# Joining the last scores of layer 0 with an AV operation, in a four-layer attention and GLU kernel with a written-out order

## The chip, the cores and the metric

The kernel runs on one core of a Trainium2 chip. The metric is the time of one execution on the device, in microseconds (us), as the median of several runs. The engines are TensorE (PE), VectorE (DVE), ScalarE (ACT), GpSimd (POOL) and SyncE (SP), which here only issues DMAs.

## The reference

Four residual layers run over x of 2048 rows by 448 columns in bf16: attention A, GLU B, then A and B again with the same weights. A has 16 heads of 28 columns; each row attends to itself and to 7 earlier rows at a distance of 2, 4, ... 14 (kg and vg below are the gathered rows). F is 1792.

```python
x = x + _A_ref(_layernorm(x, axis=-1), A_wqkv, A_wo)
x = x + _B_ref(_layernorm(x, axis=-1), B_w_gate, B_w_up, B_w_down)
x = x + _A_ref(_layernorm(x, axis=-1), A_wqkv, A_wo)
x = x + _B_ref(_layernorm(x, axis=-1), B_w_gate, B_w_up, B_w_down)

...
def _A_ref(x, wqkv, wo):
    ...
    logits = jnp.einsum("bhsd,bhswd->bhsw", q, kg) * scale
    logits = jnp.where(mask[None, None, :, :], logits, -1e9)
    attn = _softmax(logits, axis=-1)
    o = jnp.einsum("bhsw,bhswd->bhsd", attn, vg)
    return (lambda x, *d: x.transpose(*d))(o, 0, 2, 1, 3).reshape(B, S, D) @ wo
...
def _B_ref(x, w_gate, w_up, w_down):
    g = jnp.einsum("bsd,df->bsf", x, w_gate)
    u = jnp.einsum("bsd,df->bsf", x, w_up)
    h = g * u
    return jnp.einsum("bsf,fd->bsd", h, w_down)
```

## The kernel before

**Names.** The layers are li = 0 (A), 1 (B), 2 (A) and 3 (B). The rows are stored as 16 blocks of 128, four to a chunk. Even rows come first and odd rows after them, so that a distance of 2 becomes a distance of 1 and a window is a narrow band. Attention works on nine groups of queries per layer: group 0 is one query block, groups 1 to 8 are two query blocks of 120 each.

**One chunk of layer A.** Layer norm runs on DVE and ACT (L763 to L784) and gives `xn_sb`. A transpose by SP's DMA queue (L787) makes `xnTa`; in the first chunks PE does it (L794), with a copy out of PSUM (L801). Q and K are four units of 28 matmul halves (L834, tile `WQK`), copied to `qk` by ACT or DVE (L895). The last unit's columns are spread to their places by small DMAs `qk<-qk`, except in two chunks of layer 0. V is made in the same way (L834, tile `WV`), copied at L948.

**One group.** The scores are 64 small matmuls (L981) into four PSUM banks. ACT takes the exponential in two halves (L993), DVE multiplies by the band's mask (L1002), and AV is 64 small matmuls (L1020) into two banks. DVE and ACT then form the reciprocal of the row sums (L1044 to L1050, tile `R_sb`), and DVE normalises into `oT` (L1070), which gives AV's banks back. Two blocks of output projection (L854 with `wo_g`, called Y) and the addition to x (L1114) follow. In layer 2 a part of the heads is moved first by DMAs `oT<-oT`, and Y is L1106.

**One chunk of layer B.** After layer norm and transposes into `xnTb`, fourteen GLU units follow. Each is 14 matmuls (L1144) into one pair of banks; ACT copies g out (L1150) and DVE multiplies it with u (L1153) into `hT`. The down projection is 28 matmuls for two blocks (L854 with `WD`, L1165 at the very end), and DVE adds to x.

**PSUM.** There are eight banks. Nearly all operations take them in pairs and hold them until the copy, exponential, normalisation or addition that reads them has ended.

**The order.** `build` records about 1,400 operations with their dependencies in a `Sched`. The table `ORDER` has a list of operation numbers for each of PE, ACT, DVE, POOL and SP; `schedule` follows each list, one operation after the other, and hands out the banks, taking the pair that has been free longest. It also decides by its own model of time which banks those are. `emit` then writes the instructions with a wait on a semaphore for each dependency that crosses engines. Nothing overtakes on an engine: what is first in a list and not ready holds up all behind it. An operation that both ACT and DVE can do (a copy out of PSUM) is done by the one in whose list it stands.

**Tilings of PE.** Most matmuls use 64-row tiles in pairs; scores and AV use smaller tiles. Each stretch of scores or AV between other matmuls is called a visit to the small tiling.

**Joint operations.** `JOINT` has a tuple of groups for layer 0 and one for layer 2. If a group is listed, `a_chunk` does not record its AV at once, but records it together with the scores of the next group in one PE operation, by `pe_joint`: first 64 score matmuls, then 64 AV matmuls. It takes six banks together (four for the scores, two for AV) before it starts, and waits for what either part needs. In layer 2 eight groups are joined so; in layer 0 none.

Of the kernel before, what the change touches and what calls it, by code (L numbers as in the profile page):

```python
# [69 lines left out]
    ],  # L70
    "act": [
# [12 lines left out]
    ],  # L84
    "dve": [
# [19 lines left out]
    ],  # L105
    "pool": [
        23, 22, 24, 32, 19, 25, 26, 27, 18, 33, 28, 21, 20, 29, 30, 31, 34, 35, 36, 37,
    ],
# [8 lines left out]
    ],  # L117
}
ATT_P = 0.6
S_EST = 237.0  # L120
AV_EST = 241.0
A_CAP = 6
JOINT = ((), tuple(range(8)))
BPAIR = True
RESERVE = ("SV",)
RESERVE_P = 0.0
B_CAP = 8
SEQ = "A00 A01 B10 A02 B11 A03 B12 A20 B13 A21 B30 A22 B31 A23 B32 B33".split()

# [1180 lines left out]
```

## Time and profile before

| | us |
|---|---|
| median of 3 runs | 393.72 |
| lowest and highest run | 392.11 and 393.86 |
| the profiled execution | 391.6 |
| its span in the profile | 389.9 |
| PE busy in the span | 379.3 |
| DVE busy in the span | 263.8 |
| ACT busy in the span | 184.0 |

A row of a timeline has the start, the length, the engine, the line, the operation, the output and input tiles, the shapes and the number of instructions. In square brackets stand the idle time ahead of it and what ended that. Consecutive rows of the same kind are merged. The length of a row of matmuls includes the modelled end of the last one, so the distance from one row's start to the next row's start says how long the work took. A matmul of 512 columns takes about 108 ns, one of 448 columns about 94 ns, one of the small tiles about 10 ns.

### The profile page before, as it was taken

How to read it: one execution, taken by the hardware profiler on the slowest of the kernel's cores; microseconds unless marked ns; L12 is line 12 of the kernel's file. 1: busy time of each engine (PE TensorE's matmuls, PEld its weight loads, DVE VectorE, ACT ScalarE, POOL GpSimd, SP SyncE). 2: the span in 40 equal slices, each digit the busy share in tenths (PEclk: the TensorE clock that was granted, in tenths of full speed). 3: DMA queues.
4: the chain of work that ended last, by engine and by line, in shares of the span. 5: the costliest groups of instructions: out<-in, count | busy, mean ns of one | idle time of the engine just before them, and what ended most of it. 6: DMA issues, size and time to landing. Idle time of an engine off the chain costs nothing.

```text
span 389.9 us, 12779 instructions
## 1 busy us (share of the span) xinstructions
PE 379.3 (97%) x5694; PEld 201.2 (52%) x5694; DVE 263.8 (68%) x579; ACT 184.0 (47%) x302; POOL 6.0 (2%) x24
## 2 busy tenths in 40 slices
PE   7898999999999999999999999999999999999997
PEld 5454555555444555545444674445545555555554
DVE  6898879789897657355894278955478857733513
ACT  4996874772561336475143465332577303332310
POOL 6000000000000000000000000000000000000000
PEclk9999999999999999999999999999999999999999
DMA  7959675013142262000072000180001050310002
GB/s 218 266 104 159 98 128 134 3 26 74 25 72 59 30 87 57 11 6 5 5 108 43 14 6 5 24 126 5 12 2 45 19 96 13 79 41 2 13 0 96
DMA packets 53630, 22.59 MB, mean 58 GB/s; under 512 B 44288, under 2 KB 52648, under 8 KB 53576
## 3 DMA queue, kind: packets, MB, share of 16 engines
q1 hardware_dynamic: 52856, 21.15, 28.4%
q8 instruction: 45, 0.74, 0.8%
q10 hardware_dynamic: 720, 0.63, 0.5%
q14 instruction: 9, 0.07, 0.1%
HBM read 8.53 MB, written 1.84 MB: 27 GB/s over the span
## 4 chain that ended last, share of the span: by engine, by line
PE 90%; ACT 3%; DVE 3%; DMA 2%; issue 1%; SPq 1%
PE ps L1144 43%; PE ps L854 23%; PE ps L834 15%; PE ps L1106 3%; PE ps L1020 2%; PE ps L981 2%; PE ps L1165 1%; PE ps L683 1%; DMA xnTb<-xn_sb 1%; DMA qk<-qk 1%; DVE x_sb L1114 1%; ACT g_sb L1150 1%; ACT qk L895 1%; ACT E_sb L993 1%; SPq L619 1%
## 5 line engine op out<-in xcount | busy, mean ns | idle before, releaser
L1144 PE MATMUL ps<-xnTb,WGU 64*128 64x512 bf16 x1568 | 176.5, 376 | 0.8 <-DMA xnTb<-xn_sb 0.3
L1144 PEld LDWEIGHTS ps<-xnTb,WGU 64*128 64x128 bf16 x1568 | 81.1, 94 | 87.0 <-issue 4.2
L1150 ACT ACTIVATE g_sb<-ps 128x512 bf16<-128x512 f32 x112 | 64.9, 594 | 106.4 <-PE ps L1144 95.6
L1153 DVE TENSOR_TENSOR hT<-g_sb,ps 128x512 bf16<-128x512 bf16 x112 | 74.4, 681 | 51.2 <-ACT g_sb L1150 49.7
L854 PE MATMUL ps<-WD,hT 64*128 64x448 bf16 x840 | 85.7, 349 | 0.1
L854 PEld LDWEIGHTS ps<-WD,hT 64*128 64x128 bf16 x840 | 44.1, 94 | 34.6 <-DVE hT L1153 0.8
L1114 DVE TENSOR_TENSOR x_sb<-x_sb,ps 128x448 bf16<-128x448 bf16 x62 | 36.0, 614 | 30.0 <-PE ps L854 24.6
L834 PE MATMUL ps<-xnTa,WQK 64*128 64x512 bf16 (+1 forms) x448 | 47.2, 357 | 1.3 <-ACT E_sb L993 1.2
L993 ACT ACTIVATE E_sb<-ps 128x1024 bf16<-128x1024 f32 (+1 forms) x36 | 33.7, 980 | 17.9 <-PE ps L981 17.7
L763 DVE BATCH_NORM_STATS2 st<-x_sb 128x6 f32<-128x448 bf16 x64 | 38.2, 613 | 3.0 <-DMA x_sb<-in_A_x_dram 2.9
L784 DVE TENSOR_SCALAR xn_sb<-x_sb,mv,rstd 128x512 bf16<-128x512 bf16 (+1 forms) x64 | 34.8, 567 | 1.7 <-DMA xnTb<-xn_sb 1.0
L834 PEld LDWEIGHTS ps<-xnTa,WQK 64*128 64x128 bf16 x448 | 22.1, 94 | 23.0 <-ACT E_sb L993 2.7
L834 PE MATMUL ps<-WV,xnTa 64*128 64x448 bf16 (+1 forms) x252 | 28.1, 340 | 1.2 <-ACT lnv L766 0.8
L895 ACT ACTIVATE qk<-ps 128x1024 bf16<-128x1024 f32 (+1 forms) x24 | 22.8, 967 | 12.5 <-PE ps L834 12.4
L1070 DVE TENSOR_TENSOR oT<-ps,R_sb 128x448 bf16<-128x448 f32 (+2 forms) x38 | 21.1, 598 | 9.5 <-ACT R_sb L1050 9.5
L1002 DVE TENSOR_TENSOR E_sb<-E_sb,MK 128x1024 bf16<-128x1024 bf16 (+2 forms) x40 | 23.5, 604 | 3.3 <-ACT E_sb L993 3.2
L948 ACT ACTIVATE v_sb<-ps 128x896 bf16<-128x896 f32 (+1 forms) x16 | 13.7, 868 | 20.5 <-PE ps L834 20.4
L1049 ACT ACTIVATE R_sb<-R_sb 128x960 f32<-128x960 f32 (+1 forms) x18 | 17.3, 959 | 7.7 <-DVE R_sb L1047 7.5
L766 ACT ACTIVATE lnv<-mv,eps_sb 128x2 f32<-128x2 f32 (+1 forms) x34 | 9.2, 292 | 20.2 <-DVE mv L765 19.9
L834 PEld LDWEIGHTS ps<-WV,xnTa 64*128 64x128 bf16 x252 | 12.7, 94 | 11.2 <-issue 1.2
L1050 ACT ACTIVATE R_sb<-R_sb 128x960 f32<-128x960 f32 (+1 forms) x18 | 17.3, 959 | 0.4
L981 PEld LDWEIGHTS ps<-qk 28*64 28x64 bf16 x1088 | 10.1, 103 | 9.8 <-issue 4.8
(47 smaller groups left out, 172.6 us busy)
## 6 DMA issues: line engine op xcount, KB each, us to landing
out_dram<-x_sb SPq DMA_DIRECT2D x15, 112.0 KB, 1.8
WGU<-in_B_w_gate_dram SPq DMA_DIRECT2D x7, 224.0 KB, 5.1
WGU<-in_B_w_up_dram SPq DMA_DIRECT2D x7, 224.0 KB, 4.3
WD<-in_B_w_down_dram SPq DMA_DIRECT2D x14, 112.0 KB, 2.6
x_sb<-in_A_x_dram SPq DMA_DIRECT2D x3, 448.0 KB, 5.9
hT<-in_A_wqkv_dram SPq DMA_DIRECT2D x3, 224.0 KB, 5.0
qk<-qk SPq DMA_DIRECT2D x24, 28.0 KB
xnTb<-xn_sb SPq DMA_TRANSPOSE x32, 3.2
```

The lines of the kernel that those rows point to most:

```text
L763: sc.add("dve", one(lambda E, B=B: E.bn_stats(st6[:, B, :], x_sb[:, B, :]), ("bn", li, B)), 525.0, deps=[("x", li - 1, B)] + ([("xn", li - ...
L784: sc.add("dve", one(lambda E, B=B, dst=dst, src=src: E.tensor_scalar(dst, src, mv[:, B, 0:1], rstd[:, B:B + 1], ALU.subtract, ALU.mult), ( ...
L834: ins.append((lambda E, w=w, c=c, lo=lo, st=st, sp_=sp_: E.matmul(u["out"](w), u["lhs"](w, c, lo, lo + 64), u["rhs"](w, c, lo, lo + 64), s ...
L854: ins.append((lambda E, w=w, c=c, lo=lo, st=st, sp_=sp_: E.matmul(outs(w), lhs(w, c, lo), rhs(w, c, lo), start=st, stop=sp_), keys[w] if s ...
L895: return E.activation(dst, src, ACT.Copy) if hasattr(E, "activation") else E.tensor_copy(dst, src)
L993: return E.activation(E_sb[:, slot, 2 * hp:2 * hp + 2, 0:w], ps[:, b0:b0 + 2, 0:w], ACT.Exp, scale=SCALE)
L1002: return E.tensor_tensor(e, e, m, ALU.mult)
L1070: return E.tensor_tensor(dst, src, rec, ALU.mult)
L1114: sc.add("dve", one(lambda E: E.tensor_tensor(x_sb[:, B, :], x_sb[:, B, :], ps[:, bk[w], 0:D], ALU.add), ("x", li, B)), dve_est(D), deps=[ ...
L1144: ins.append((lambda E, u=u, k=k, w=w: E.matmul(u["out"](w), WGU[64 * w:64 * w + 64, k, 128 * u["fc"]:128 * u["fc"] + 128], X[64 * w:64 * ...
L1150: sc.add("act", one(lambda E, gs=gs, bk=bk: E.activation(g_sb[:, gs, 0:n], ps[:, bk[0], 0:n], ACT.Copy), ("G", li, jp, fc)), act_est(n), d ...
L1153: sc.add("dve", one(lambda E, gs=gs, bk=bk, fc=fc: E.tensor_tensor(hT[:, fc, hs, h0:h1], g_sb[:, gs, 0:n], ps[:, bk[1], 0:n], ALU.mult), ( ...
```

## The change

Group 7 of layer 0 is listed in `JOINT`, so that AV of group 7 and the scores of group 8 become one operation. The number of operations falls by one, and all five lists of `ORDER` are replaced. No matmul is added or removed.

```diff
-JOINT = ((), tuple(range(8)))
+JOINT = ((7,), tuple(range(8)))
...
     "pe": [
-        280, 277, 281, 278, 283, 391, 261, 262, 392, 300, 288, 395, 397, 396, 393, 398, 394, 407, 305, 408, 296, 410, 297, 523, 411, 527, 524, 521, 528,
+        280, 277, 281, 278, 283, 391, 261, 392, 262, 300, 288, 395, 397, 396, 398, 393, 394, 305, 407, 296, 408, 297, 410, 523, 411, 527, 524, 521, 528,
...
```

Where it moves instructions is shown by rows of each engine's program, in order; "x" and a number at the end is how many alike stand in a row.

The first place is SP's queue between the loads of the weights and the Q/K work of chunk 2 of layer 0. L787 is the transpose of one block of that chunk, `WGU` are halves of the GLU weights (224 KB), `wo_g` pieces of the output projection (98 KB). Before:

```order
L619 DMA wo_g<-in_A_wo_dram 28x4x448
L787 DMA_TRANSPOSE xnTa<-xn_sb 128x4x128
L619 DMA WGU<-in_B_w_up_dram 64x1792
L787 DMA_TRANSPOSE xnTa<-xn_sb 128x4x128 x2
L619 DMA WGU<-in_B_w_up_dram 64x1792
L787 DMA_TRANSPOSE xnTa<-xn_sb 128x4x128
L619 DMA WGU<-in_B_w_up_dram 64x1792
```

Now:

```order
L619 DMA WGU<-in_B_w_up_dram 64x1792
L787 DMA_TRANSPOSE xnTa<-xn_sb 128x4x128
L619 DMA wo_g<-in_A_wo_dram 28x4x448
L619 DMA WGU<-in_B_w_gate_dram 64x1792 x2
L619 DMA wo_g<-in_A_wo_dram 28x4x448
L787 DMA_TRANSPOSE xnTa<-xn_sb 128x4x128 x3
L619 DMA WGU<-in_B_w_gate_dram 64x1792 x2
```

Four loads now stand between the first transpose and the three others, which follow each other directly; before, one load stood behind the first and one ahead of the last.

The second place is PE behind the scores of group 2 of layer 0 (the first row of each piece). `WQK` is Q and K of chunk 2, `wo_g` two blocks of Y. Before:

```order
L981 MATMUL ps<-qk 64x64 x64
L834 MATMUL ps<-xnTa,WQK 128x512 x6
L854 MATMUL ps<-wo_g,oT 128x448 x16
L834 MATMUL ps<-xnTa,WQK 128x512 x8
L981 MATMUL ps<-qk 64x64 x64
L1020 MATMUL ps<-E_sb,v_sb 32x64 x64
```

Now:

```order
L981 MATMUL ps<-qk 64x64 x64
L834 MATMUL ps<-xnTa,WQK 128x512 x6
L854 MATMUL ps<-wo_g,oT 128x448 x8
L834 MATMUL ps<-xnTa,WQK 128x512 x8
L854 MATMUL ps<-wo_g,oT 128x448 x8
L981 MATMUL ps<-qk 64x64 x64
L1020 MATMUL ps<-E_sb,v_sb 32x64 x64
```

The two halves of Y stood next to each other; now eight Q/K matmuls stand between them.

The third place is PE around the joint operation. `WD` are down matmuls, L1144 GLU units, L981 scores and L1020 AV; the last rows of scores and AV of layer 0 are among them. Before:

```order
L854 MATMUL ps<-WD,hT 128x448 x14
L1144 MATMUL ps<-xnTb,WGU 128x512 x14
L854 MATMUL ps<-WD,hT 128x448 x28
L981 MATMUL ps<-qk 64x64 x64
L1144 MATMUL ps<-xnTb,WGU 128x512 x42
L1020 MATMUL ps<-E_sb,v_sb 32x64 x64
L1144 MATMUL ps<-xnTb,WGU 128x512 x70
```

Now:

```order
L854 MATMUL ps<-WD,hT 128x448 x14
L981 MATMUL ps<-qk 64x64 x64
L1144 MATMUL ps<-xnTb,WGU 128x512 x14
L854 MATMUL ps<-WD,hT 128x448 x28
L981 MATMUL ps<-qk 64x64 x64
L1020 MATMUL ps<-E_sb,v_sb 32x64 x64
L1144 MATMUL ps<-xnTb,WGU 128x512 x42
L1020 MATMUL ps<-E_sb,v_sb 32x64 x64
L1144 MATMUL ps<-xnTb,WGU 128x512 x70
```

Scores of group 8 are followed by AV of group 7 without anything between them; scores of group 7 come later than before, behind the down matmuls.

Some copies out of PSUM change their engine. In layer 2, four of Q/K (two of chunk 0, one each of chunks 1 and 3) and four of V go from ACT to DVE, and two of Q/K of chunk 3 from DVE to ACT; in the head, one copy of a transpose goes from DVE to ACT, and of four copies that arrange the Q/K weights two go each way.

More of the change, by code (lines that the diff above doesn't have):

```diff
@@ L55 @@
     "pe": [
[14 rows of a table removed]
[14 rows of a table added]
     ],
     "act": [
[12 rows of a table removed]
[11 rows of a table added]
     ],
     "dve": [
[19 rows of a table removed]
[20 rows of a table added]
     ],
     "pool": [
-        23, 22, 24, 32, 19, 25, 26, 27, 18, 33, 28, 21, 20, 29, 30, 31, 34, 35, 36, 37,
+        21, 24, 32, 28, 33, 29, 23, 25, 26, 22, 27, 19, 34, 35, 30, 31, 20, 18, 36, 37,
     ],
     "sp": [
[7 rows of a table removed]
[7 rows of a table added]
     ],
```

102 rows, old and new, of the table ORDER are left out of this document.

## The prediction, made before the result was known

> **What bounds the kernel now.** I read the page first (engine totals, slices, chain), then PE's and SP's timelines, then the rows around each place where the order changes.
>
> ```profile
> span 389.9 us, 12779 instructions
> PE 379.3 (97%) x5694; PEld 201.2 (52%) x5694; DVE 263.8 (68%) x579; ACT 184.0 (47%) x302; POOL 6.0 (2%) x24
> PE 90%; ACT 3%; DVE 3%; DMA 2%; issue 1%; SPq 1%
> ```
>
> PE is busy for 379.3 of 389.9 us and 90% of the chain. The joint operation issues the same 64 score and 64 AV matmuls as before, so PE's work doesn't shrink. What can move is its idle time, 389.9 - 379.3 = 10.6 us, and what hides inside busy time: slower matmuls at a change of tiling, and waits shorter than a matmul. The table of stretches says where the idle time lies (length, then PE, PEld, DVE and ACT busy):
>
> ```profile
> 0.00:20.00 20.00, 16.56 (x310) 9.78 (x312) 15.48 (x49) 13.73 (x30) 6.04 (x24) 1.00 0.90 241
> 20.00:40.00 20.00, 18.06 (x427) 9.06 (x425) 18.15 (x50) 16.23 (x25) 0.00 (x0) 1.00 0.75 129
> 40.00:56.00 16.00, 15.69 (x335) 8.32 (x333) 12.94 (x35) 12.71 (x17) 0.00 (x0) 1.00 0.75 110
> 80.00:112.00 32.00, 31.84 (x544) 16.46 (x542) 28.49 (x60) 15.33 (x25) 0.00 (x0) 1.00 0.27 48
> 286.00:295.00 9.00, 8.14 (x279) 4.50 (x279) 7.04 (x17) 7.42 (x9) 0.00 (x0) 1.00 0.04 11
> ```
>
> Before 20 us PE waits for loads, which keep their order up to the weights of layer 0. From 20 to 56 us 1.94 + 0.31 = 2.25 us are idle, with ACT and DVE close to full; where the join is put (80 to 112) only 0.16. So the join has little to win by itself, and the new order of the first 56 us has more.
>
> **The change part by part.** *Transposes of chunk 2 (28 to 33 us).* These PE and SP rows carry the largest term; the view of xnT in that window adds, last, the time of its transposes to landing; the last row is of the page's DMA issues.
>
> ```profile
> 30.38 0.84 PE L981 MATMUL ps<-qk 28*64 28x64 bf16 x64 [0.46 <-DVE v_sb L948]
> 32.37 0.82 PE L834 MATMUL ps<-xnTa,WQK 64*128 64x512 bf16 x6 [1.15 <-ACT E_sb L993]
> 33.02 1.94 PE L854 MATMUL ps<-wo_g,oT 64*128 64x448 bf16 x16
> 34.79 1.03 PE L834 MATMUL ps<-xnTa,WQK 64*128 64x512 bf16 x8
> 21.88 1.29 SPq L787 DMA_TRANSPOSE xnTa<-xn_sb  x1
> 27.57 0.59 SPq L619 DMA_DIRECT2D WGU<-in_B_w_up_dram  x1
> 28.21 2.41 SPq L787 DMA_TRANSPOSE xnTa<-xn_sb  x1
> DMA to landing us min/median/max: 2.5/4.3/5.8
> WD<-in_B_w_down_dram SPq DMA_DIRECT2D x14, 112.0 KB, 2.6
> ```
>
> The scores of group 2 need 0.64 us (a score row further below runs from 102.47 to 103.11), so PE is through at 30.38 + 0.64 = 31.02 and stands until 32.37: 1.35 us. The row names ACT's exp, but that had no part in it: the operation that starts there is the first Q of chunk 2, and the last input it needs is the transpose issued at 28.21, behind the load of 27.57, 4.16 us before, near the median of 4.3. In the new order one transpose goes at about 21.9, then four loads of 0.6 each, then the other three back to back: 21.9 + 1.3 + 4 x 0.6 = 25.6, and at 1.3 each the third is issued at about 28.2, with no load between. It lands 2.5 us later (the shortest of the row) at 30.7, 4.3 us later at 32.5, or 5.8 us later at 34.0. PE, itself about 0.35 late from the head (by ACT's rows taken in the new order: copies of T now stand behind a Q copy of 1.0), gets there at 31.02 + 0.35 = 31.37. The first Q would so start at 31.4, 32.5 or 34.0, against 32.37. The 5.8 is that of a transpose with four loads of 224 KB just ahead of it; here the four are two of 224 and two of 98 KB, and the third transpose has two others in front of it, which give the loads 2.6 us to drain. I take 31.6: **-0.75** with the head in it, bounds -1.0 and +1.6.
>
> [...]
>
> *Y halves and the first GLU unit (33 to 56 us).* The 16 matmuls of L854 above take 34.79 - 33.02 = 1.77 us, two halves of 8 that write one pair of banks, where 16 such matmuls need 1.51 at 94.5 ns each (14 take 280.28 - 278.95 = 1.33 in the rows on bank waits below): 0.26 lost. The new order puts eight Q matmuls between them: **-0.25** (bounds -0.26, 0). The stretch ends at a transpose:
>
> ```profile
> 51.55 4.01 DMA xnTb<-xn_sb
> 54.75 0.74 PE L834 MATMUL ps<-WV,xnTa 64*128 64x448 bf16 x6
> 55.80 1.47 PE L1144 MATMUL ps<-xnTb,WGU 64*128 64x512 bf16 x12 [0.31 <-DMA xnTb<-xn_sb]
> ```
>
> Between the V of 54.75 (6 steps of 94.5 = 0.57, so done at 55.32) and the GLU unit of 55.80 lie 0.48 us, for the last of four xnTb transposes. They now follow the qk copies directly, and the Y and x additions behind them come earlier by what was won above, so the wait doesn't come back whole: **-0.3** (bounds -0.5, 0). Together 0 to 56: **-1.3**.
>
> *Around the join (74 to 110 us).*
>
> ```profile
> 96.56 1.49 PE L854 MATMUL ps<-WD,hT 64*128 64x448 bf16 x14
> 98.21 1.69 PE L1144 MATMUL ps<-xnTb,WGU 64*128 64x512 bf16 x14 [0.16 <-ACT rstd L768]
> 99.73 2.81 PE L854 MATMUL ps<-WD,hT 64*128 64x448 bf16 x28
> 102.47 0.71 PE L981 MATMUL ps<-qk 28*64 28x64 bf16 x64
> 103.11 4.71 PE L1144 MATMUL ps<-xnTb,WGU 64*128 64x512 bf16 x42
> 107.75 0.68 PE L1020 MATMUL ps<-E_sb,v_sb 64*32 64x64 bf16 x64
> ```
>
> Joining saves one visit to the small tiling. 28 down matmuls ahead of scores take 102.47 - 99.73 = 2.74 us, 28 x 94.5 ns are 2.64: 0.10 a visit. **-0.10**. 14 down matmuls need 1.32, so PE is free at 97.88 and waits 0.33 for a transpose until 98.21; that one is issued earlier now: **-0.33** (bound 0). Against it: the joint operation takes six of the eight banks at once (scores two pairs, AV one), so the second GLU unit behind it waits until its exp or its x addition frees a pair: +0.17, from 0 to +1.0 (one pass of ACT over a pair of banks, as in rival C). And it can't start before the masked exp of group 7, whose second half ACT now does behind a G copy; by the ACT and DVE rows it is ready at about 101.45, PE is there at 101.5. No wait is counted; what is queued behind it is the whole of PE. With +0.06 for two down halves set next to each other: **-0.2** (bounds -0.45, +1.0).
>
> *Bank waits in GLU units.* A unit that follows only one other since its banks' owner waits for the chain G copy, H multiply:
>
> ```profile
> 247.34 16.95 PE L1144 MATMUL ps<-xnTb,WGU 64*128 64x512 bf16 x154
> 264.11 5.48 PE L834 MATMUL ps<-xnTa,WQK 64*128 64x512 bf16 x56
> 277.43 1.69 PE L1144 MATMUL ps<-xnTb,WGU 64*128 64x512 bf16 x14
> 278.95 1.49 PE L854 MATMUL ps<-WD,hT 64*128 64x448 bf16 x14
> 280.28 0.73 PE L834 MATMUL ps<-WV,xnTa 64*128 64x448 bf16 x6
> ```
>
> A free unit takes 278.95 - 277.43 = 1.52; eleven in a row 264.11 - 247.34 = 16.77, 0.15 above 11 x 1.51, one such wait. Following the new order bank by bank, one of these goes (near 70 us), and four come (two in layer 1, two in layer 3): **-0.15 + 0.60** (bounds -0.15, +0.9).
>
> *Copies that change engine.* Most PSUM copies that move go from ACT to DVE, among them the first two Q/K casts of layer 2:
>
> ```profile
> 132.04 1.82 DVE L895 CAST qk<-ps 128x512 bf16<-128x512 f32 x2 [1.22 <-PE ps L834]
> 133.78 1.38 DVE L784 TENSOR_SCALAR xn_sb<-x_sb,mv,rstd 128x896 bf16<-128x896 bf16 x2
> 139.48 1.15 DVE L1114 TENSOR_TENSOR x_sb<-x_sb,ps 128x448 bf16<-128x448 bf16 x2 [4.33 <-PE ps L854]
> 141.84 0.34 PE L981 MATMUL ps<-qk 28*64 28x72 bf16 x32
> 163.72 3.51 DMA qk<-qk
> ```
>
> Two casts of 1.2 us more go into a row behind which DVE had nothing to do for 4.33 us. The last cast ends at about 135; the last qk copy is issued by about 137.1 and lands 3.5 us later at 140.6, 0.7 before the scores of 141.84 - 0.5 need it. Cost **0**; without that cover it is one for one.
>
> *Layer 3, 286 to 295 us.*
>
> ```profile
> 290.09 1.68 PE L1144 MATMUL ps<-xnTb,WGU 64*128 64x512 bf16 x14
> 292.53 0.71 PE L981 MATMUL ps<-qk 28*64 28x64 bf16 x64 [0.77 <-ACT g_sb L1150]
> ```
>
> The unit of 290.09 should end at 291.6; the scores wait 0.93, to 292.53, for a normalisation that holds their banks. The new order puts a GLU unit straight behind the AV ahead of it, which waits 0.54 for a pair that an exp still reads, but this eats most of the 0.93: **+0.15** (bounds -0.3, +0.54).
>
> Sum: -1.3 - 0.2 - 0.15 + 0.60 + 0.15 = **-0.9**. The profiled execution took 391.6 with 1.7 around its span; 390.7 then, and the runs' median of 393.72 lies 2.12 above the profiled one, so **392.8**.
>
> **The rivals.**
>
> *A, late transposes, small gain.* The third transpose lands as late as now, 32.4, as batches behind loads do; then the first Q starts where it did, and only the later terms stay: -0.9 + 0.75 = about -0.1, **393.6**. For it: median 4.3. Against: no load between the three.
>
> *B, the searched order removes the waits of 20 to 56 us nearly all.* Those are the 2.25 us idle of the table and 0.26 within Y; with them gone, the join at its lower bound (-0.45) and half of the new bank waits not there, -2.5 - 0.45 + 0.15 = -2.8 against the profile, **390.9**. For it: ACT's and DVE's queues were both rearranged, and each wait there is short. Against: ACT is 81% busy from 20 to 40 us, and something has to wait for it.
>
> *C, slower: transposes behind the loads at 5.8 us.* At 34.0 the first Q is 1.6 late, and R of group 2, whose two passes now both stand ahead of a Q copy on ACT, holds that copy's banks for one pass more:
>
> ```profile
> 39.79 1.00 ACT L895 ACTIVATE qk<-ps 128x1024 bf16<-128x1024 f32 x1
> 40.69 0.99 ACT L1050 ACTIVATE R_sb<-R_sb 128x960 f32<-128x960 f32 x1
> ```
>
> That is +1.6 in place of -0.75 and 1.0 for the pass: -0.9 + 2.35 + 1.0 = +2.4, **396.2**. It decides from a landing later than 33.5 on. Against: transposes of 5.8 us had twice the bytes ahead. [...]
>
> **How the numbers follow.** The forecast 0.45, A 0.15, B 0.23, C 0.17. Faster by over 0.5% means under 391.75, slower over 395.7; within lies what a measurement of this kernel can't tell from no change. B gives 0.2 of faster and the forecast's lower edge 0.1: 0.30. C gives 0.13 of slower, and unlisted waits 0.03: 0.16. The rest, 0.54, is same. The forecast's own range, by its bounds, is 391.3 to 394.2; to leave 2 in 10 out the whole reaches from 390.4 (a little below B) to 395.4 (short of the full price of C).
>
> **What would show it.** The first Q of chunk 2 at 31.4 to 32.0 instead of 32.37 and no row of 16 matmuls at L854 near 33 (step one and two); the first GLU unit of L1144 at 54.2 to 54.9; one stretch of scores and AV back to back near 101 with a GLU unit after it whose successor waits under 0.3; DVE casts of qk near 132 to 135 and scores near 141 without a wait on qk; a wait under 0.6 at the scores near 292. Wrong is the forecast if the first GLU unit comes after 55.8, if the joint operation is waited for by more than 0.3, or if scores of layer 2 show a wait on qk beyond that at 167.36 now.

## The result, and the profile after

The changed kernel takes 394.27 us in the median of 20 runs (392.15 to 396.81), the kernel before, run beside it, 392.50 (391.36 to 394.52): a ratio of 1.0037 [1.0021, 1.0054]. A second comparison of the same two kernels, e9 below, gave 1.0014 [0.9997, 1.0031]. So the change costs between nothing and 2 us. A gain of 0.9 had been forecast; the time lies within the range given and within 0.5% of the kernel before, but on the other side of it.

The page of the changed kernel, its span and its engine totals:

```profile
span 391.5 us, 12764 instructions
PE 379.7 (97%) x5694; PEld 202.5 (52%) x5694; DVE 269.5 (69%) x584; ACT 179.9 (46%) x297; POOL 5.8 (1%) x24
```

The span is 1.6 us longer than before (391.5 - 389.9), and PE's busy time is 0.4 longer; the other 1.2 are idle time of PE. The table of stretches says where (length, then PE, PEld, DVE and ACT busy, as before):

```profile
20.00:40.00 20.00, 17.40 (x449) 9.20 (x436) 18.07 (x50) 16.45 (x27) 0.00 (x0) 1.00 0.79 131
40.00:56.00 16.00, 15.41 (x327) 8.11 (x326) 12.94 (x30) 12.18 (x17) 0.00 (x0) 1.00 0.70 102
80.00:112.00 32.00, 31.89 (x594) 16.33 (x573) 27.25 (x61) 16.25 (x25) 0.00 (x0) 1.00 0.24 46
```

From 20 to 56 us PE now idles 2.60 + 0.59 = 3.19 us, against 2.25 before. Around the join it idles 0.11, as little as before. PE's timeline shows the place:

```profile
32.50 0.82 PE L834 MATMUL ps<-xnTa,WQK 64*128 64x512 bf16 x6 [1.03 <-DMA xnTa<-xn_sb]
33.14 0.94 PE L854 MATMUL ps<-wo_g,oT 64*128 64x448 bf16 x8
33.90 1.04 PE L834 MATMUL ps<-xnTa,WQK 64*128 64x512 bf16 x8
34.76 0.94 PE L854 MATMUL ps<-wo_g,oT 64*128 64x448 bf16 x8
35.63 0.71 PE L981 MATMUL ps<-qk 28*64 28x64 bf16 x64
36.27 0.75 PE L1020 MATMUL ps<-E_sb,v_sb 64*32 64x64 bf16 x64
36.95 2.01 PE L834 MATMUL ps<-xnTa,WQK 64*128 64x512 bf16 x19
40.53 2.55 PE L834 MATMUL ps<-xnTa,WQK 64*128 64x512 bf16 x23 [1.57 <-issue]
```

The scores of group 3 start at 35.63, still 0.12 ahead of the kernel before (35.75, below). Then the 42 Q/K matmuls, one row of 4.68 us before, fall into 19 and 23 with 1.57 us between them, and the bracket names no engine, no tile and no DMA, only "issue". That is the row to stop at. The 23 read the same tiles as the 19, and the stop lies within a unit of 14, so missing data is unlikely. Before, the same row was whole, in PE's timeline of the kernel before:

```profile
35.75 0.71 PE L981 MATMUL ps<-qk 28*64 28x64 bf16 x64
37.00 4.68 PE L834 MATMUL ps<-xnTa,WQK 64*128 64x512 bf16 x42
```

What could be missing is the instructions. The page's table of DMA queues has a kind that it calls instruction; the larger of its two queues is q8 (packets, MB, share of the engines):

```profile
q8 instruction: 45, 0.74, 0.8%
```

0.74 MB in 45 packets are 16 KB each; PE's 5,694 matmuls and 5,694 weight loads over 45 packets are 253 instructions a packet. By this count the author takes q8 to bring PE's code, one block a packet; no record names what is in one. Windows cut around the stop catch a single packet. The table of queues of the changed kernel for 37.95 to 39.20 us:

```profile
q1 hardware_dynamic: 294, 0.07, 259.3%
q8 instruction: 1, 0.02, 6.0%
```

And of the kernel before for 36.95 to 38.15:

```profile
q1 hardware_dynamic: 493, 0.12, 149.2%
q8 instruction: 1, 0.02, 5.8%
```

The packets' own records give 37.98 to 39.17 in the changed kernel and 36.99 to 38.10 before. So the code came 1.0 us later in the span, and 1.1 later against the start of the scores of group 3. PE resumed 1.36 us behind its end. Queue q1, which carries SP's transposes and weight loads, has a share above 100% in both (259.3 and 149.2), so the times of its packets overlap. SP's timeline of the changed kernel ahead of that packet:

```profile
23.44 2.34 SPq L619 DMA_DIRECT2D WGU<-in_B_w_gate_dram  x2
25.82 0.58 SPq L619 DMA_DIRECT2D wo_g<-in_A_wo_dram  x1
26.44 4.66 SPq L787 DMA_TRANSPOSE xnTa<-xn_sb  x3
31.15 1.24 SPq L619 DMA_DIRECT2D WGU<-in_B_w_gate_dram  x2
32.43 1.88 SPq L619 DMA_DIRECT2D WGU<-in_B_w_up_dram  x3
```

Five halves of the GLU weights, 224 KB each, go out in one piece from 31.15 to 34.31. Before there were four, from 30.66 to 33.18, in SP's timeline of the kernel before:

```profile
30.66 0.59 SPq L619 DMA_DIRECT2D WGU<-in_B_w_up_dram  x1
31.30 0.60 SPq L619 DMA_DIRECT2D WGU<-in_B_w_gate_dram  x1
31.94 0.60 SPq L619 DMA_DIRECT2D WGU<-in_B_w_up_dram  x1
32.58 0.60 SPq L619 DMA_DIRECT2D WGU<-in_B_w_gate_dram  x1
```

The ledger of the two profiles, by PE's rows:

| place | before | after | change in this stretch |
|---|---|---|---|
| first Q of chunk 2 | 32.37 | 32.50 | +0.13 |
| scores of group 3 | 35.75 | 35.63 | -0.25 |
| end of the 42 Q/K matmuls behind them | 41.68 | 43.08 | +1.52 |
| first GLU unit | 55.80 | 57.03 | -0.17 |
| end of the span | 389.9 | 391.5 | +0.35 |

### The profile page after: what moved, and what is told of

It is laid out like the page before. It is cut to its first block, busy times and chain, and to the rows that moved or that the text cites. A ratio compares the mean times of both kernels' runs of the same rounds, so it can differ in the third digit from the quotient of the medians.

```text
span 391.5 us, 12764 instructions
## 1 busy us (share of the span) xinstructions
PE 379.7 (97%) x5694; PEld 202.5 (52%) x5694; DVE 269.5 (69%) x584; ACT 179.9 (46%) x297; POOL 5.8 (1%) x24
## 4 chain that ended last, share of the span: by engine, by line
PE 89%; DVE 4%; ACT 3%; DMA 2%; issue 1%; SPq 1%
PE ps L1144 41%; PE ps L854 24%; PE ps L834 14%; PE ps L1106 3%; PE ps L981 2%; PE ps L1020 2%; PE ps L683 1%; PE ps L1165 1%; DMA qk<-qk 1%; DMA xnTa<-xn_sb 1%; ACT xnTa L801 1%; DVE E_sb L1002 1%; DVE R_sb L1047 1%; DVE R_sb L1045 1%; ACT E_sb L993 1%
## 5 line engine op out<-in xcount | busy, mean ns | idle before, releaser
L1144 PE MATMUL ps<-xnTb,WGU 64*128 64x512 bf16 x1568 | 176.3, 376 | 1.6 <-ACT E_sb L993 0.5
L1144 PEld LDWEIGHTS ps<-xnTb,WGU 64*128 64x128 bf16 x1568 | 82.2, 94 | 86.3 <-issue 5.3
L834 PE MATMUL ps<-xnTa,WQK 64*128 64x512 bf16 (+1 forms) x448 | 47.3, 356 | 2.7 <-issue 1.6
L784 DVE TENSOR_SCALAR xn_sb<-x_sb,mv,rstd 128x896 bf16<-128x896 bf16 (+1 forms) x64 | 35.5, 574 | 2.5 <-ACT rstd L768 1.7
L834 PEld LDWEIGHTS ps<-xnTa,WQK 64*128 64x128 bf16 x448 | 22.5, 94 | 23.7 <-issue 3.4
L834 PE MATMUL ps<-WV,xnTa 64*128 64x448 bf16 (+1 forms) x252 | 28.3, 339 | 0.6 <-DVE hT L1153 0.3
L895 ACT ACTIVATE qk<-ps 128x1024 bf16<-128x1024 f32 (+1 forms) x22 | 21.4, 988 | 13.7 <-PE ps L834 13.6
L834 PEld LDWEIGHTS ps<-WV,xnTa 64*128 64x128 bf16 x252 | 12.1, 94 | 11.6 <-PE ps L834 1.6
L895 DVE CAST qk<-ps 128x1024 bf16<-128x1024 f32 (+1 forms) x10 | 10.1, 1008 | 9.9 <-PE ps L834 9.7
L948 ACT ACTIVATE v_sb<-ps 128x896 bf16<-128x896 f32 (+1 forms) x12 | 10.2, 851 | 13.6 <-PE ps L834 13.6
```

The lines of the kernel that those rows point to most:

```text
L784: sc.add("dve", one(lambda E, B=B, dst=dst, src=src: E.tensor_scalar(dst, src, mv[:, B, 0:1], rstd[:, B:B + 1], ALU.subtract, ALU.mult), ( ...
L834: ins.append((lambda E, w=w, c=c, lo=lo, st=st, sp_=sp_: E.matmul(u["out"](w), u["lhs"](w, c, lo, lo + 64), u["rhs"](w, c, lo, lo + 64), s ...
L895: return E.activation(dst, src, ACT.Copy) if hasattr(E, "activation") else E.tensor_copy(dst, src)
L1144: ins.append((lambda E, u=u, k=k, w=w: E.matmul(u["out"](w), WGU[64 * w:64 * w + 64, k, 128 * u["fc"]:128 * u["fc"] + 128], X[64 * w:64 * ...
```

## The experiments

PE's matmuls are counted from the program's start, the first being 0. The 19 Q/K matmuls end with number 728, and 729 is the late one. "Stop" below is the time from the start of 728 to that of 729; the two start together, at 0.00, in the profiles of e5, e7, e8 and e12, in which no stop is seen. "Code" is the start of the q8 packet ahead of it, the fifth in each profile, from the packets' records.

**First round: is it the head, the join, or the code?** *e1* keeps the change but has SP's first 45 DMAs in the order of before.

```diff
-"sp": ..., 190, 196, 97, 105, 110, 102, 104, 214, 216, 210, 212, 103, ...
+"sp": ..., 192, 110, 101, 108, 109, 214, 210, 216, 103, 212, ...
```

> The changed kernel with the first 45 DMAs of SP's queue (weights, transposes and qk copies of layer 0, transposes of the first chunk of layer 1) in the order that they had before; all else as changed. Theory (late code): PE stops for 1.6 us inside the Q/K of chunk 2 because the load of its next instructions, asked for at about 35 us, stands behind the five weight loads that SP now issues in one piece; with the old queue it starts 1 us earlier and the stop shrinks to under 0.6 us: 1.0 to 1.5 us faster than the changed kernel, about 1.001 of the kernel before. Rival (banks): the stop is for banks held by the Q/K copy that ACT now does behind both passes of R of group 2; then it stays and the time stays at 1.004 of before. Rival (later order): the loss is behind 60 us; then nothing changes here either.

Measured: 398.34 us, ratio 1.0139 [1.0109, 1.0169]. The stop was gone, but the run says little: the first Q waited far longer for its transposes, as PE's timeline shows,

```profile
36.12 1.47 PE L776 MATMUL ps<-xnTa,WQK 64*128 64x512 bf16 x6 [4.11 <-DMA xnTa<-xn_sb]
```

(L776 is the L834 of the other listing; the experiments' order tables take fewer lines). SP's old order asks for blocks of `xn_sb` in an order in which the new DVE list doesn't make them: the first transpose of chunk 2 went out at 26.57, where it had gone at 21.48. A miss, and a reminder that one engine's list can't be swapped alone.

*e2* puts 24 short matmuls more into PE's warm-up (5,718 matmuls and as many weight loads in its page), which shifts all later code by 48 instructions against the work and touches no order.

```diff
+        if n == WARM + FILL - 1:
+            ins = [... matmul of 64 columns on the warm-up tile ... for k in range(24)] + ins
```

> The changed kernel with 24 more matmuls of 64 columns in the last warm-up operation at about 11 us, whose result nobody reads; all orders as changed. It moves every later instruction of PE by 48 places against the blocks in which code is loaded. Late code: the block's end comes before the scores of group 2, where PE stands for transposes anyway, so the next load is asked for 2 us or more earlier against the work; the stop of 1.6 us near 39 us goes, and at most 0.6 us are paid for the 24 matmuls: 0.8 to 1.6 us faster than the changed kernel, about 1.000 of before. Banks, or later order: the stop stays where it is in the work (behind 19 Q/K matmuls), and the time is that of the changed kernel or up to 0.6 us more.

Measured: 395.27 us, 1.0058 [1.0033, 1.0084]. No gain, but the rows of PE's timeline are the clearest of the study:

```profile
36.97 0.75 PE L964 MATMUL ps<-E_sb,v_sb 64*32 64x64 bf16 x59
39.45 0.21 PE L964 MATMUL ps<-E_sb,v_sb 64*32 64x64 bf16 x5 [1.72 <-issue]
39.59 4.22 PE L778 MATMUL ps<-xnTa,WQK 64*128 64x512 bf16 x42
```

The stop left the Q/K row, which is whole again, and moved 24 matmuls ahead in the work, into the AV: five AV matmuls and nineteen Q/K ones now lie behind it that lay ahead of it. Its number is still 729. What PE waits for thus hangs on the count of its instructions, not on any tile: a wait for data, a bank or a semaphore is out. The same kernel had a second such stop of 1.56 us, to 228.85, in the down matmuls of layer 1; there too a q8 packet had just ended, at 227.39.

*e3* takes every operation that starts ahead of the first GLU unit in its old order, on all engines, and the rest, join included, in the new one.

```diff
-ORDER: all lists of the change
+ORDER: the 392 operations up to the first GLU unit as in before, the others as in the change
```

> Everything that the kernel before starts ahead of the first GLU unit (392 operations, all engines) stands in its old order, everything behind it in the new order, with the join. Late code, or banks: the loss lies in the first 56 us, so this one is as fast as before within 0.4 us plus what the later order costs (+0.3 by the two profiles): 1.000 to 1.002. Later order: it is as slow as the changed kernel, 1.004.

Measured: 391.86 us, 0.9988 [0.9968, 1.0008], stop 0.47, code at 35.70. With the old head the loss goes.

*e4* takes the join apart and leaves the rest.

```diff
-JOINT = ((7,), tuple(range(8)))
+JOINT = ((), tuple(range(8)))
...
-"pe": ..., 568, ...
+"pe": ..., 580, 568, ...
```

> The changed kernel with the joint operation taken apart again: scores of group 8 and AV of group 7 stand next to each other in PE's list, as two operations, each with its own waits and banks; all orders as changed. If the join itself costs or wins next to nothing, as predicted (one visit to the small tiling is saved by the place, not by the operation): the changed kernel within 0.3 us. If taking six banks at once costs PE a wait: up to 1 us faster than the changed kernel, with scores that start earlier than 101.8 us.

Measured: 393.07 us, 1.0011 [0.9989, 1.0033], stop 2.14. PE's rows at the place of the join, without it:

```profile
102.14 0.71 PE L923 MATMUL ps<-qk 28*64 28x64 bf16 x64
102.77 0.68 PE L962 MATMUL ps<-E_sb,v_sb 64*32 64x64 bf16 x64
103.45 2.76 PE L1086 MATMUL ps<-xnTb,WGU 64*128 64x512 bf16 x24
```

And in the changed kernel:

```profile
102.45 0.71 PE L981 MATMUL ps<-qk 28*64 28x64 bf16 x64
103.09 0.68 PE L1020 MATMUL ps<-E_sb,v_sb 64*32 64x64 bf16 x64
103.77 4.71 PE L1144 MATMUL ps<-xnTb,WGU 64*128 64x512 bf16 x42
108.40 0.68 PE L1020 MATMUL ps<-E_sb,v_sb 64*32 64x64 bf16 x64
```

From scores to GLU unit 1.31 us apart, 1.32 joined. The order already sets the two side by side, and joining them adds nothing and costs nothing.

**Second round: do the loads in one piece make the code late?** *e5* puts all six weight loads behind the four transposes of chunk 3 in the changed kernel, *e6* only two of the five that stood ahead.

```diff
-"sp": ..., 97, 105, 110, 102, 104, 214, 216, 210, 212, 103, ...
+e5:   ..., 214, 216, 210, 212, 97, 105, 110, 102, 104, 103, ...
+e6:   ..., 97, 105, 110, 214, 216, 210, 212, 102, 104, 103, ...
```

(97 to 110 are weight halves, 210 to 216 the transposes.)

> The changed kernel with one difference, in SP's queue: the five weight loads that it issues in one piece at about 31 us (and the sixth) stand behind the four transposes of chunk 3 instead of ahead of them. Banks and all other orders are those of the changed kernel. Late code behind weight loads: the load of PE's next instructions, asked for at about 35 us, starts at 37.2 or earlier instead of 38.0, and the stop at matmul 729 (1.9 us from the matmul ahead of it) shrinks to under 1.0: 0.7 to 1.5 us faster than the changed kernel. If the transposes delay it as much as loads do: start at 37.5 or later, stop over 1.5, no change. If the stop has nothing to do with DMA traffic: 1.9 as before.

> As the kernel of the run ahead, but only the last two of the five loads (and the sixth) stand behind the transposes. Late code behind loads: between the changed kernel and the run ahead, a stop of 1.0 to 1.6. Otherwise: 1.9.

e5: 392.85 us, 0.9996 [0.9979, 1.0014]. The stop was gone (0.00), and with the transposes alone ahead of it the code came at 35.81, 0.10 ahead of the scores, so no delay by these is seen. But a new wait took part of the gain. Its PE timeline, where chunk 3's scores of group 4 stand:

```profile
51.58 0.70 PE L923 MATMUL ps<-qk 28*64 28x64 bf16 x64 [1.36 <-DMA qk<-qk]
```

And SP's timeline of e5:

```profile
42.24 1.88 SPq L561 DMA_DIRECT2D WGU<-in_B_w_up_dram  x3
44.16 0.60 SPq L561 DMA_DIRECT2D WGU<-in_B_w_gate_dram  x1
44.87 2.19 SPq L561 DMA_DIRECT2D qk<-qk  x3
```

The small copies that these scores need now stand behind six loads. e6: 391.77 us, 0.9974 [0.9960, 0.9989], stop 0.10, and no wait there. Three loads are left in the piece ahead of the transposes, in SP's timeline of e6:

```profile
30.61 2.13 SPq L561 DMA_DIRECT2D WGU<-in_B_w_gate_dram  x2
32.79 0.60 SPq L561 DMA_DIRECT2D WGU<-in_B_w_up_dram  x1
```

*e7* asks the reverse: the kernel before with five loads in one piece. *e8* is e3 with all its loads behind the transposes.

```diff
-"sp" of before: ..., 110, 101, 108, 109, 214, 210, 216, 103, 212, ...
+e7:             ..., 110, 101, 108, 109, 103, 214, 210, 216, 212, ...
+e8, on e3:      ..., 214, 210, 216, 212, 110, 101, 108, 109, 103, ...
```

> The kernel before with one difference, in SP's queue: the weight load that stood among the transposes of chunk 3 is issued with the four ahead of them, so that five go in one piece, as in the changed kernel. Late code behind loads: the gap at matmul 729, 0.49 in the profile of before, grows to 0.8 to 1.6, and the time by 0.3 to 1.1 us (1.001 to 1.003). If the piece of five is not the cause: 0.5 and 1.000.

> The kernel with the old order up to the first GLU unit and the new one behind it (0.9988 of before), and with all five weight loads around the transposes of chunk 3 moved behind these. Late code behind loads: the gap at matmul 729 goes from 0.47 to 0.2, and the transposes land earlier: 0.2 to 0.8 us faster than without the move, about 0.997 of before. If loads that land later hold up the first GLU units, or the traffic only moves: no change or slower.

e7: 392.89 us, 1.0012 [0.9997, 1.0027], and no stop in its profile (0.00): a miss for the theory by that profile, and inconclusive by the time. e8: 392.71 us, 0.9996 [0.9977, 1.0015], stop 0.00, but as in e5 the scores of group 4 then waited for the copies behind the loads (0.68 us), and nothing was left of the gain.

**Third round: repeats and the remaining halves.** *e9* is the changed kernel unaltered. *e10* has the changed head and the old order behind it, without the join; *e11* is e6 with the join apart; *e12* is e3 with two loads ahead of the transposes and three behind.

```diff
+e10: the operations up to the first GLU unit as in the change, the others as in before, JOINT = ((), ...)
+e11: e6 with JOINT = ((), ...), "pe": ..., 580, 568, ...
+e12, on e3, "sp": ..., 110, 101, 214, 210, 216, 212, 108, 109, 103, ...
```

> The changed kernel, unaltered, beside the three that follow. Late code: PE stops again at matmul 729, 1.7 to 2.2 us from the matmul ahead of it, with the load of its code starting at 37.8 or later; 1.003 to 1.005 of before. If the stop of the first profile was a single case: under 1.0 us, and the slowness lies elsewhere.

> The counterpart of e3: what the changed kernel starts ahead of the first GLU unit in its new order, everything behind it in the old order, without the join. Late code in the first 56 us: as slow as the changed kernel or 0.3 us less, 1.003 to 1.004, with the stop at matmul 729. If the loss needs the later order or the join: 1.000.

> The kernel of e6 (two of five loads behind the transposes, 0.9974 of before) with the joint operation taken apart, as e4 did with the changed kernel. The join costs nothing: 0.997, as e6. The join costs 1 us, as the medians of e4 and the changed kernel (393.1 and 394.3) could be read: 0.995, and scores of group 8 that start earlier.

> The kernel of e3 (old order up to the first GLU unit, new behind it) with the weight loads split as in e6: two ahead of the transposes of chunk 3, three behind them. e8 put all behind, which took the gap at matmul 729 away and made one of 1.05 us at matmul 902, where the next block of code comes in. Late code behind loads: neither gap, 0.3 to 1 us faster than e3, 0.995 to 0.998 of before. Otherwise 0.999.

(The "next block of code" named for e8 in the last of these was a misreading: that wait is on the qk copies.) e9: 393.21 us, 1.0014 [0.9997, 1.0031], stop 2.03. e10: 395.21 us, 1.0053 [1.0033, 1.0072], stop 1.65: the changed head alone brings the loss, without the join and without the new tail. e11: 391.75 us, 0.9981 [0.9961, 1.0000], stop 0.39: beside e6, the join is again worth nothing. e12: 392.09 us, 0.9983 [0.9957, 1.0008], stop 0.00.

**Fourth round: the dose.** *e13* repeats e7, *e14* puts six loads in one piece in the kernel before, *e15* repeats e6.

```diff
+e14, "sp" of before: ..., 110, 101, 108, 109, 103, 104, 214, 210, 216, 212, ...
```

> The kernel of e7, unaltered (the kernel before with five weight loads in one piece). In the profile of e7 a stretch of half clock made PE 1.3 us later against the loads, so that it could not tell. Late code behind loads: in a profile without such a stretch the code load starts at 37.5 or later and the gap at matmul 729 is 0.8 to 1.6; 1.001 to 1.003 of before. If five in one piece are not enough by themselves: under 0.6 and 1.000.

> The kernel before with six weight loads in one piece ahead of the transposes of chunk 3 (the one among them and the one among the qk copies are moved up). Late code behind loads: the code load starts at 38.5 or later, the gap at matmul 729 is 1.5 to 3, the time 0.8 to 2 us above before (1.002 to 1.005). Otherwise as before.

> The kernel of e6, unaltered: the order of the changed kernel with two of the five loads moved. If 0.9974 was no chance: 0.996 to 0.999 of before, no gap over 0.6 at matmul 729.

e13: 393.15 us, 1.0011 [0.9994, 1.0029], this time with a stop of 1.37. e14: 394.95 us, 1.0051 [1.0029, 1.0074], stop 1.83. Its PE timeline has the same 19 and 23, now in the old order of PE:

```profile
37.37 2.21 PE L776 MATMUL ps<-xnTa,WQK 64*128 64x512 bf16 x19
41.04 2.32 PE L776 MATMUL ps<-xnTa,WQK 64*128 64x512 bf16 x23 [1.46 <-issue]
```

e15: 392.17 us, 0.9986 [0.9971, 1.0001], stop 0.38. In PE's timeline of e15 the row is whole:

```profile
36.74 4.56 PE L776 MATMUL ps<-xnTa,WQK 64*128 64x512 bf16 x42
```

All runs that bear on the stop, with the weight loads that stand in one piece ahead of chunk 3's transposes (times in us; "scores" is the start of matmul 582, the first score of group 3; in e2 number 582 stands 24 matmuls ahead of those scores):

| kernel | loads ahead | scores | code, start | after the scores | stop | ratio to before |
|---|---|---|---|---|---|---|
| before | 4 | 35.75 | 36.99 | 1.24 | 0.49 | 1 |
| e3, old head | 4 | 34.59 | 35.70 | 1.11 | 0.47 | 0.9988 |
| e12, old head | 2 | 34.88 | 35.22 | 0.34 | 0.00 | 0.9983 |
| e8, old head | 0 | 35.23 | 35.10 | -0.13 | 0.00 | 0.9996 |
| e5, the change | 0 | 35.91 | 35.81 | -0.10 | 0.00 | 0.9996 |
| e7, before | 5 | 37.12 | 37.64 | 0.52 | 0.00 | 1.0012 |
| e13, the same | 5 | 37.28 | 39.36 | 2.08 | 1.37 | 1.0011 |
| e14, before | 6 | 36.09 | 38.72 | 2.63 | 1.83 | 1.0051 |
| the change | 5 | 35.63 | 37.98 | 2.35 | 1.94 | 1.0037 |
| e9, the same | 5 | 36.49 | 39.06 | 2.57 | 2.03 | 1.0014 |
| e4, join apart | 5 | 35.15 | 37.87 | 2.72 | 2.14 | 1.0011 |
| e10, old tail | 5 | 36.49 | 38.46 | 1.97 | 1.65 | 1.0053 |
| e2, shifted | 5 | 33.85 | 36.83 | 2.98 | 1.92 | 1.0058 |
| e1, SP as before | 4 | 40.60 | 41.22 | 0.62 | 0.16 | 1.0139 |
| e6, the change | 3 | 36.75 | 36.93 | 0.18 | 0.10 | 0.9974 |
| e15, the same | 3 | 35.36 | 36.27 | 0.91 | 0.38 | 0.9986 |
| e11, join apart | 3 | 35.75 | 36.05 | 0.30 | 0.39 | 0.9981 |

In every profile with a stop of more than 1 us PE resumes 1.2 to 1.5 us behind the end of the packet, and in none of the 17 does matmul 729 start less than 1.2 us behind it. The stop follows the packet's start, and the packet's start follows the loads, with a spread: with five loads the packet may come in time (e7) or late (e13) in one and the same kernel. A stretch of half clock, with which the expectation of e13 explains e7, isn't the difference, since e13 had one too (mean granted clock 0.996 in e7's profile, 0.995 in e13's).

The records of queue q1 tie the two together. A weight half moves in packets of 3,584 bytes, and the last of those issued ahead of the transposes ended at 36.30 in the kernel before, 37.98 in the changed one, 38.04 in e14 and 35.60 in e6; the code started 0.69, 0.00, 0.68 and 1.33 us later. In e7 they ended at 37.18 and in e13 at 38.15, which is 1.0 of the 1.7 us between the starts of their code; the rest is open. Of the 15 profiles with loads ahead, only e2 has the code start before the loads have ended (36.83, against 39.23).

## Why the prediction was wrong

**The step that failed** is one that isn't in it: the sum has no term for PE's own code. The prediction follows data, banks and DMAs and has nothing for 36 to 43 us. The price of that stretch was +1.52, nearly the whole 1.6 by which the span grew, and 1.45 of it is the stop, which grew from 0.49 to 1.94; the other stretches together came to +0.06. Shown: the stop keeps its number when the work is shifted (e2), it goes with the loads when these are thinned out (e6, e11, e15, e12; e5 and e8 at another price), and it grows in the old order when loads are added (1.83 with six in e14; with five, e13 has it and e7 doesn't). Not shown: when the sequencer asks for its packet (about 35 us in the expectations of e1 and e5, the end of a block in that of e2: the author's assumptions); with no loads ahead (e5, e8) it starts 0.1 us before matmul 582. That the packet waits behind SP's loads in the DMA engines is concluded from its start and from theirs, and no record splits the start into asking and waiting.

That the time still lies within the range is luck: the range was drawn for late transposes and bank waits, and neither made the loss. The range of 391.3 to 394.2 that the prediction takes from its bounds isn't what these add up to either: that is 391.1 to 397.8.

**Transposes of chunk 2, -0.75.** Measured +0.13. The three transposes did go out together and the third landed 3.36 us after its issue, a row of the chain of waits:

```profile
29.01 3.36 DMA xnTa<-xn_sb
```

That landing would have been enough; the issue was late. "25.6" for SP's being through with the loads took four at 0.6; the two gate halves took 2.34 together in place of 1.2, and the rest was on time. Why a load's issue takes longer in some places wasn't tried. Runs of one and the same order differ as much: the first Q of chunk 2 came at 32.37 in the kernel before and at 31.20 in e3, which has the same order there. A term of that size can't be read from a single profile.

**Y halves, -0.25.** Right: 3.13 us from the first Q to the scores of group 3 where it was 3.38, and no row of 16.

**First GLU unit, -0.3.** Half right. The wait between the V and the unit, 0.48 before, shrank by 0.18, to 57.03 - 56.16 - 0.57 = 0.30, by PE's timeline of the changed kernel:

```profile
56.16 0.74 PE L834 MATMUL ps<-WV,xnTa 64*128 64x448 bf16 x6
57.03 1.69 PE L1144 MATMUL ps<-xnTb,WGU 64*128 64x512 bf16 x14
```

The place was wrong, 57.03 and not 54.2 to 54.9, because the stop lies ahead of it and the first Q came no earlier.

**Around the join, -0.2.** The work from the AV at 78.69 to the GLU row at 118.95 took 40.26 us before; the same work takes 39.98 now (79.77 to 119.75), a gain of 0.28. The wait of 0.33 for a transpose is gone: the unit that had it starts at 98.19, straight behind scores. The two risks named, banks for the second unit behind it and the masked exp, didn't come: three GLU units behind it take 108.40 - 103.77 = 4.63 us, as they did before (107.75 - 103.11). Of the join itself 0.10 had been expected, for a visit saved. e4 and e11 leave scores and AV side by side, so they show that the joint operation adds nothing to that; what the saved visit is worth by itself wasn't tried.

**Bank waits, -0.15 + 0.60.** Too high. The GLU units that wait 0.15 for their banks became one more, where a net of three more had been counted.

**Copies of layer 2, 0.** Right: the two casts run on DVE from 131.17, and the scores at 142.27 wait for nothing.

**Layer 3, +0.15.** Measured about +0.04 (286.30 to 292.53 before, 287.88 to 294.15 now, from the AV to the scores), by the mechanism named. PE's timeline of the changed kernel:

```profile
289.09 1.69 PE L1144 MATMUL ps<-xnTb,WGU 64*128 64x512 bf16 x14 [0.53 <-ACT E_sb L993]
294.15 0.70 PE L981 MATMUL ps<-qk 28*64 28x64 bf16 x64 [0.27 <-DVE oT L1070]
```

The unit straight behind the AV waits 0.53 (0.54 forecast), and the scores' 0.93 shrinks to 294.15 - 292.20 - 1.52 = 0.43.

All terms behind 60 us were forecast at +0.40 together and came to +0.35, in part by luck: an unlisted +0.29 around the scores near 232 us, whose cause wasn't looked for, makes up for the bank waits that stayed away. Nearly all of the miss of 2.5 us in the profile lies in the head: 0.88 in the transposes and 1.52 in the code.

**The rivals.** By its time A (393.6) lies nearest to 394.27; by the change, 1.6 in the profile, C (+2.4) does. C's place, a wait in the Q/K work of chunk 2, was almost right, but its mechanism didn't happen: the transposes landed after 3.36 us, not 5.8, and no bank was waited for. A describes the first Q of chunk 2 (32.50, where A has 32.37), not the loss behind it. B's 2.25 us of waits from 20 to 56 were not won: they became 3.19.

The best kernel is e6, the change with two loads moved: 0.9974 and, repeated, 0.9986 of before. By these ratios it leads the changed kernel (1.0037 and 1.0014) by 1.1 to 2.5 us; its stop, 0.10 and 0.38 against 1.94, is 1.6 to 1.8 us shorter, which is about that lead.

## What to carry to other kernels

When a row of PE breaks in two with "issue" between, count the matmuls up to it and look for the instruction packet in the queue table of that window. In e2 a shift of the count by 24 matmuls moved the break 24 matmuls through the work and left it at number 729: such a break hangs on PE's instructions and not on a tile. The 64 scores and 64 AV matmuls ahead of the 42 Q/K matmuls, 256 instructions with their weight loads against the 253 of a packet, took 1.32 us in the changed kernel (35.63 to 36.95). So, as the author reads it, in this kernel the stretch after such short matmuls is where big loads should not stand in one piece: the profiles with up to four at a time had a stop of 0.49 us at most, those with five or six one of 0.00 (e7) to 2.14 (e4). Loads that are moved back must not land ahead of small copies that are due: the scores waited 1.36 us for these in e5 and 0.68 in e8.

## What the runs showed of the hardware

Beside the code packets, the clock was not what it had seemed. In 8 of the 15 experiments' profiles the mean granted clock was 0.995 or 0.996, in the other seven 1.000. In e9 and e2, whose tables of stretches were read there, PE ran at half clock for a while from about 20 us on, and e9 is the changed kernel, whose first profile shows no such stretch. PE's timeline of e9, then its table of stretches (the granted clock stands behind the five engines):

```profile
20.53 4.67 PE L834 MATMUL ps<-xnTa,WQK 64*128 64x512 bf16 x28
```

```profile
16.00:20.00 4.00, 2.48 (x108) 1.42 (x105) 3.93 (x11) 3.75 (x7) 0.00 (x0) 1.00 0.93 212
20.00:22.00 2.00, 2.00 (x72) 1.03 (x58) 2.00 (x7) 2.00 (x6) 0.00 (x0) 0.53 0.06 17
22.00:24.00 2.00, 2.00 (x14) 0.73 (x12) 1.96 (x6) 1.24 (x3) 0.00 (x0) 0.61 0.33 70
```

At a clock of 0.5, the lowest granted in such a table (22 to 24 us of e2), 0.53 and 0.61 over 2 us each come to (0.94 + 0.78) / 0.5 = 3.4 us at half clock, an estimate; the granted 0.78, 0.50 and 0.87 of e2 from 20 to 26 us give the same. The same 28 matmuls take 3.20 us in the changed kernel's first profile, in which the clock stayed at 1.00. The stretch costs about 1.5 us (4.67 - 3.20), comes and goes from run to run of one kernel (the change without it, e9 with it), and is as large as the effect studied: it is a good part of why the two comparisons of the change differ. In the runs whose mean granted clock was 1.00 the changed kernel took 393.1 in both (6 of 20 runs, then 9 of 12), and the kernel before, in the runs beside the experiments, 392.1 to 392.5; so at full clock the change costs about 0.7 to 1.1 us. It follows a stretch from 16 to 20 us in which PE is busy only 2.48 of 4 us, but the changed kernel's first profile has the same 2.48 there and kept its clock, as its table of stretches shows:

```profile
16.00:20.00 4.00, 2.48 (x133) 1.59 (x130) 3.98 (x12) 3.94 (x7) 0.00 (x0) 1.00 0.99 216
```

What brings the stretch on was not shown.
